# From two phases to one pipeline: normalised attention followed by a cosine MLP, on one core

## The chip, the cores and the metric

The kernel runs on one core of one Trainium2 chip. The metric is the time on the device in microseconds (us). Engines: TensorE (PE in the profile; its weight loads are PEld), VectorE (DVE), ScalarE (ACT), GpSimd (POOL) and SyncE (SP, which here only starts DMAs). Lower is better.

## The reference, cut to what matters

```python
q, k, v: (8 batches, 12 heads, 448 tokens, 64)     # float32
q_n = q / norm(q);  k_n = k / norm(k)
attn = softmax(q_n @ k_n.T / 0.1)                   # |score| <= 10
x = (attn @ v) with the heads side by side          # (3584, 768)
h = x @ w_in                                        # w_in (768, 2048)
out = (h * cos(h)) @ w_out                          # w_out (2048, 768)
```

The scores are bounded by 10, so both kernels leave out the subtraction of the maximum. The matrix products run in bf16.

## The kernel before

It has two phases, one after the other. The attention goes head by head (96 heads, loaded in 16 units of six). The keys and queries are scaled by GpSimd and transposed by TensorE. Scores are made transposed (keys on partitions), so that the exponentials can be the moving operand of the AV product. The weights of AV are 128 columns: 64 of V and 64 of ones. So partitions 64 to 127 of the result hold the softmax sum, 64 times over, and VectorE can invert and multiply.

```python
def norm(g):                         # VectorE, once per head
    vec.wait_ge(s_av, g + 1)
    vec.reciprocal(rtmp[gp].ap()[D : 2 * D, :], AV[gp].ap()[D : 2 * D, :]) ...   # 64 x 448
    vec.tensor_tensor(xt_dst, AV[gp].ap()[0:D, :], rtmp[gp].ap()[D : 2 * D, :], ALU.mult) ...

# TensorE, per head: 4 AV matmuls, 4 score matmuls of the next head, 8 transposes
for g in range(NG):
    emit_av(g)
    if g + 1 < NG: emit_sc(g + 1)
    if g + 3 < NG: emit_tp(g + 3)

# then, in a second block with its own buffers: the MLP
for sb in range(NSB + 1):            # 7 blocks of 512 tokens
    if sb < NSB: m1(sb)              # 96 matmuls of 512 columns, cos on ScalarE, product on VectorE
    if sb >= 1:  m2(sb - 1)          # 128 matmuls of 384 columns
```

## Time and profile before

The time is 840.8 us (840.4 to 840.9).

| what | value | where it is read |
|---|---|---|
| attention | 0 to about 520 us | timeline |
| MLP | about 520 to 839 us | timeline |
| VectorE busy, 130 to 330 us | 179 of 200 us | windows |
| TensorE busy, 520 to 840 us | 301 of 320 us | windows |
| reciprocals | 96 x 2.96 us = 284 us | groups |

The first two columns after the stretch in a line of the windows view are its length and TensorE's busy time. Then follow the other engines, the recorded clock, and the share and rate of the DMA engines. Kernel before:

```profile
130.00:330.00 200.00, 161.02 (x617) 70.18 (x616) 179.05 (x127) 121.41 (x142) 56.30 (x24) 1.00 0.31 81
520.00:840.00 320.00, 301.30 (x1568) 145.85 (x1568) 79.31 (x114) 101.00 (x141) 0.00 (x0) 1.00 0.12 35
```

In the attention VectorE is the full engine. In the MLP it is TensorE.

The groups show VectorE's work per head: line, engine, operation, output and input, count, then busy time in total and the mean in ns of one, then what it waited for. Kernel before:

```profile
L237 DVE RECIPROCAL rtmp<-AV 64x448 f32<-64x448 f32 x96 | 284.2, 2960 | 44.1 <-PE AV L352 39.8
L241 DVE TENSOR_TENSOR xT<-AV,rtmp 64x448 bf16<-64x448 f32 x96 | 59.3, 618 | 3.3
L228 DVE COPY qkT_sb<-TP 64x896 bf16<-64x896 bf16 x96 | 58.7, 612 | 12.7 <-PE TP L323 11.1
```

The page's slices (40 equal parts of the span, tenths of busy time; PEclk is the granted clock) for the kernel before:

```profile
PE   0797797797797797797797797999999999999997
PEclk9999999999999999999999999999999999999999
```

And its timeline of TensorE, the transposes of one head (start, length, operation; x4 is four instructions merged):

```profile
302.13 0.58 PE L319 MATMUL TP<-ident,qs 112*64 112x112 bf16 x4
302.50 0.58 PE L323 MATMUL TP<-ident,kb 112*64 112x112 bf16 x4
```

Four transposes of 112 columns take from 302.13 to 302.50, that is 1.2 columns per ns. In the MLP 128 matmuls of 384 columns take 20.80 us (chain of waits), that is 2.36 columns per ns. So the attention ran at half TensorE's rate, although the clock row reads 9 everywhere. The trace holds no clock record before 525.5 us, and the row shows full speed where nothing was recorded. **The spacing of matmuls is the better clock.**

### The profile page before, as it was taken

Reading aid. Unit: us, or ns where it says so; the run is one execution under the profiler, and the core shown is the slowest. Engines: PE = TensorE matmul, PEld = TensorE weight load, DVE = VectorE, ACT = ScalarE, POOL = GpSimd, SP = SyncE. Lnnn points to the kernel's source line nnn. Section 1 sums busy time; section 2 is a strip of 40 time slices with the busy share of each in tenths; the row PEclk is TensorE's granted clock in tenths of the full one; section 3 lists DMA queues with packets and bytes.
Section 4 is the critical chain, followed back from the end, with each engine's and each line's share of the span. In section 5 each row is a group of like instructions: output and inputs, shape, how many; then the busy total and the mean of one; then the engine's idle time right before and its main releaser. Section 6 shows DMA issues by size and latency. Waiting matters only on the chain. (4 is left out here: it accounts for less than half of the span.)

```text
span 838.7 us, 7918 instructions
## 1 busy us (share of the span) xinstructions
PE 706.1 (84%) x3104; PEld 321.0 (38%) x3104; DVE 535.0 (64%) x438; ACT 407.3 (49%) x494; POOL 132.1 (16%) x60
## 2 busy tenths in 40 slices
PE   0797797797797797797797797999999999999997
PEld 0343243243243243243333342335454444445464
DVE  3698898898898898898898898441312223131400
ACT  4656656656656656756755733442323333232311
POOL 3434124124113113213213200000000000000000
PEclk9999999999999999999999999999999999999999
DMA  9761452364033043034040000001111020102022
GB/s 286 209 198 61 115 174 80 94 174 89 10 100 99 1 98 97 3 98 98 2 99 0 1 0 1 1 0 39 38 37 39 20 56 20 57 1 76 0 76 76
DMA packets 40516, 57.13 MB, mean 68 GB/s; under 512 B 1824, under 2 KB 34080, under 8 KB 39712
## 3 DMA queue, kind: packets, MB, share of 16 engines
q1 hardware_dynamic: 40480, 56.63, 24.5%
q8 instruction: 25, 0.41, 0.2%
q14 instruction: 11, 0.09, 0.0%
HBM read 45.61 MB, written 11.01 MB: 68 GB/s over the span
## 5 line engine op out<-in xcount | busy, mean ns | idle before, releaser
L237 DVE RECIPROCAL rtmp<-AV 64x448 f32<-64x448 f32 x96 | 284.2, 2960 | 44.1 <-PE AV L352 39.8
L290 ACT ACTIVATE expT<-SCP 112x896 bf16<-112x896 f32 x192 | 165.4, 913 | 165.4 <-PE SCP L337 165.4
L337 PE MATMUL SCP<-qkT_sb 64*112 64x448 bf16 x384 | 166.8, 587 | 56.3 <-DVE qkT_sb L228 54.2
L486 DVE TENSOR_TENSOR gT<-PH,cosh 128x512 bf16<-128x512 f32 x112 | 77.5, 692 | 194.7 <-ACT cosh L459 194.7
L352 PE MATMUL AV<-expT,vp 112*128 112x448 bf16 x384 | 160.5, 572 | 35.4 <-ACT expT L290 34.3
L425 PE MATMUL PH<-xT,W 128*128 128x512 bf16 x672 | 156.5, 383 | 14.7 <-DVE gT L486 10.8
L440 PE MATMUL PO<-W,gT 128*128 128x384 bf16 x896 | 146.6, 326 | 0.0
L337 PEld LDWEIGHTS SCP<-qkT_sb 64*112 64x112 bf16 x384 | 65.7, 200 | 161.1 <-DVE qkT_sb L228 118.6
L459 ACT ACTIVATE cosh<-PH,cst 128x512 f32<-128x512 f32 x112 | 77.0, 688 | 88.3 <-PE PH L425 88.3
L440 PEld LDWEIGHTS PO<-W,gT 128*128 128x128 bf16 x896 | 87.7, 98 | 58.6
L425 PEld LDWEIGHTS PH<-xT,W 128*128 128x128 bf16 x672 | 58.2, 98 | 112.0 <-DVE gT L486 51.0
L177 POOL TENSOR_TENSOR kb<-Kf,rk 112x1536 bf16<-112x1536 f32 x16 | 44.2, 2762 | 340.9 <-ACT rk L281 340.9
L468 ACT ACTIVATE out_sb<-PO 128x768 f32<-128x768 f32 x28 | 22.7, 811 | 123.6 <-PE PO L440 123.6
L352 PEld LDWEIGHTS AV<-expT,vp 112*128 112x128 bf16 x384 | 38.4, 126 | 97.6 <-issue 55.2
L319 PE MATMUL TP<-ident,qs 112*64 112x112 bf16 x384 | 55.7, 301 | 21.7 <-POOL qs L180 21.6
L319 PEld LDWEIGHTS TP<-ident,qs 112*64 112x64 bf16 x384 | 35.3, 158 | 83.6 <-issue 83.6
L228 DVE COPY qkT_sb<-TP 64x896 bf16<-64x896 bf16 x96 | 58.7, 612 | 12.7 <-PE TP L323 11.1
L241 DVE TENSOR_TENSOR xT<-AV,rtmp 64x448 bf16<-64x448 f32 x96 | 59.3, 618 | 3.3
L323 PE MATMUL TP<-ident,kb 112*64 112x112 bf16 x384 | 55.8, 301 | 0.0
L180 POOL TENSOR_TENSOR qs<-Qf,rq 112x1536 bf16<-112x1536 f32 x16 | 44.2, 2762 | 0.0
L323 PEld LDWEIGHTS TP<-ident,kb 112*64 112x64 bf16 x384 | 43.9, 177 | 0.0
L273 ACT ACT_TABLE_LOAD x16 | 20.5, 1283 | 37.8 <-DVE qn L215 37.8
(25 smaller groups left out, 233.5 us busy)
## 6 DMA issues: line engine op xcount, KB each, us to landing
Qf<-in_q_dram SPq DMA_DIRECT2D x16, 672.0 KB, 5.5
Kf<-in_k_dram SPq DMA_DIRECT2D x16, 672.0 KB, 8.5
Vf<-in_v_dram SPq DMA_DIRECT2D x16, 672.0 KB, 9.9
wstage<-in_moe_w_in_dram SPq DMA_DIRECT2D x6, 1024.0 KB, 8.3
wstage<-in_moe_w_out_dram SPq DMA_DIRECT2D x4, 1536.0 KB, 6.7
out_dram<-out_sb SPq DMA_DIRECT2D x8, 336.0 KB, 2.6
out_dram<-out_sb SPq DMA_DIRECT2D x8, 288.0 KB, 2.6
out_dram<-out_sb SPq DMA_DIRECT2D x8, 240.0 KB, 2.5
```

The lines of the kernel that those rows point to most:

```text
L228: vec.tensor_copy(qkT_sb[gp].ap(), TP[gp].ap()).then_inc(s_ev, 1)
L237: vec.reciprocal(rtmp[gp].ap()[D : 2 * D, :], AV[gp].ap()[D : 2 * D, :]).then_inc(s_vself, 1)
L241: vec.tensor_tensor(xt_dst, AV[gp].ap()[0:D, :], rtmp[gp].ap()[D : 2 * D, :], ALU.mult).then_inc(s_dv, 1)
L290: act.activation(dst, src, ACT.Exp).then_inc(s_exp, 1)
L319: last = pe.transpose(TP[gp].ap()[0:D, NP * j : NP * (j + 1)], qs[i].ap()[:, col : col + D], ident.ap())
L323: last = pe.transpose(TP[gp].ap()[0:D, S + NP * j : S + NP * (j + 1)], kb[i].ap()[:, col : col + D], ident.ap())
L337: ins = pe.matmul(outap, lhsT, rhs, start=True, stop=True)
L352: ins = pe.matmul(AV[gp].ap(), lhsT, rhs, start=(j == 0), stop=(j == NJ - 1))
L425: ins = pe.matmul(PH[t % 2].ap(), W1v[:, c, 128 * nb : 128 * nb + 128], xTv[:, c, MB * sb : MB * sb + MB], start=(c == 0), stop=(c == NKC ...
L440: ins = pe.matmul(PO[T2 % 2].ap()[:, 512 * n2h : 512 * n2h + N2W], gTv[sbp % 2][:, f, 128 * ms : 128 * ms + 128], W2v[:, f, N2W * n2h : N2 ...
L459: act.activation(cosh[t % 2].ap(), PH[t % 2].ap(), ACT.Sin, bias=cst.ap()[:, 1:2], scale=1.0).then_inc(s_cos, 1)
L486: vec.tensor_tensor(gTv[sb % 2][:, nb, :], PH[t % 2].ap(), cosh[t % 2].ap(), ALU.mult).then_inc(s_gm, 1)
```

## The change: intent and diff

The new kernel is a small program builder (operations with the tiles that they read and write, semaphores worked out from that) and one pipeline over 16 units of six heads:

- Heads go in pairs. Scores of a pair are two 64-row tiles of the array, AV of a pair two 64-column tiles; both are meant to run side by side.
- The softmax sums come from matmuls with 32 columns of ones. ScalarE evicts AV and sums to SBUF. A gather DMA spreads a unit's 2688 sums over 128 partitions by 21 columns; VectorE adds the two halves and inverts. A DMA writes the result to DRAM, and two more read it back, copied to 64 partitions each. These three DMA steps are called the hops below.
- The MLP runs under the attention. First-layer matmuls of a batch (two units) come as one burst every second unit. Second-layer matmuls fill in by 4 to 6 in each of a unit's 12 quanta (a quantum is one score chunk of a pair). Weights are cast by the DMA.

The core of the diff, with cuts (lines of the kernel before that it takes out are those shown above):

```diff
+    def av_step(g, c):                    # one chunk of keys, both heads
+        for a in range(2):
+            r = slice(64 * a, 64 * a + 64)
+            k = slice(0, 128) if c < NC3 else r
+            ... matmul(AVv[r, 0, 0:S], vav[i][k, 8*p + (4*a + c if c < NC3 else NC3), :], px, start=(c == 0), stop=(c == NC3))
+    def av_sums(g):
+        for c in (0, 1, 2, 3):
+            for a in range(2):
+                o = slice(64 * a + 32 * (c % 2), 64 * a + 32 * (c % 2) + 32)
+                ... matmul(AVv[o, 1, 0:S], ones.ap()[k, :], px, start=(c < 2), stop=(c >= 2))
+        ... ACT Copy xuv[i][:, :, p, :] <- AVv[:, :, 0:S]
+    def gather(u):    ... 4 DMAs  sums[i] (128 x 42) <- xu
+    def recip(u):     ... DVE add of the halves, DVE reciprocal, 128 x 21
+    def spread(u):    ... DMA  scr (DRAM) <- rcp
+    def broadcast(u): ... 2 DMAs  RB (64 partitions each) <- scr
+    def normalise(u, p): ... DVE xT <- xu * RB
...
+            if u == 0 and kq >= 2 or u == 1:
+                load_w(1)                                  # POOL's DMA queue, with the cast
...
+            if per_quantum:
+                m2_fill(per_quantum[kq % len(per_quantum)])
+            if g >= 1:
+                if c in (1, 2):
+                    av_step(g - 1, 2 * c - 2)
+                    av_step(g - 1, 2 * c - 1)
+                if c == 2: av_sums(g - 1)
+                if kq == 3: gather(u - 1)
+            if u % 2 == 1 and u >= 3 and kq == M1_AT:       # M1_AT = 2
+                m1((u - 3) // 2)
...
+            fills = (4,) if b % 2 == 0 else (6, 5, 5)
```

## The prediction

> **What bounds the kernel now.** The windows view splits the 838.7 us span: 0-30 us start, 30-520 us attention, 520-839 us MLP. In 330-520 us VectorE is busy 173.5 of 190 us: attention is VectorE-bound. Per head (groups): reciprocal over 64 partitions 2960 ns, eviction of transposes 612, multiply 618, plus 3.5 us of reductions per unit; in all about 4.8 us x 96 heads. In the MLP TensorE is the chain (chain of waits: L440 17%, L425 11% of the span); 128 second-layer matmuls take 20.8 us (162 ns each, 384 columns), a 12-matmul pair of first-layer groups 2.97 us where 12 x 216 ns would be 2.6.
>
> The timeline also shows 448-column attention matmuls starting 373 ns apart (1.2 columns/ns), though the page says granted clock 1.0; the MLP streams 384 columns in 162 ns (2.4 columns/ns). The Trainium skill ("TensorE: Matmul & The Clock Gate", part 1) describes a half-rate state until the array has been busy for some 3.4 us; this trace agrees with the rates: attention, with TensorE never saturated, runs at half.
>
> **What the change does.**
> - Removes the 2960 ns reciprocal (284 us in total): 16 small ones over 21 columns instead, plus two hops through DRAM that have several us of slack.
> - VectorE per pair: eviction 0.61, reduction about 1.1, normalise 0.62; MLP multiplies 64 x 1.09, output evictions 56 x 0.5. Total about 220 us (535 now).
> - ScalarE: per pair 3 x 0.91 + 0.54 exponentials and 0.91 eviction, 4.2 us, 201 us; sines 64 x 1.0; table loads about 17 x 1.28 (66 now). About 300 us.
> - GpSimd: squares, scaling, casts about 3.7 us per pair, 180 us, below ScalarE.
> - The MLP runs under the attention, so TensorE becomes the bound, and stays at full rate.
>
> **TensorE, estimated at 2.4 columns/ns.** MLP 768 x 189 ns + 896 x 162 ns = 291 us. Per pair: 7 transposes 0.5; scores and AV as two concurrent tiles each, 0.8 + 0.8; sums 0.65; about 2.75 us. Tile-shape switches: the trace's gaps from one matmul kind to the next are 0.12-0.18 us at half rate; I take 0.08 x 13 per pair = 1.05. So 3.8 x 48 = 182 us. That tiles overlap is from the skill ("TensorEngine Tiling (Array Packing)", Tiling Modes, key properties); no trace yet shows it. If they don't, pairs cost 1.8-2 us more, about +90 us.
>
> Sum: first scores 10; TensorE 473; three first units without MLP work, limited by ScalarE or by a half-rate TensorE, +12; waiting for weights (18 MB wanted in 55 us) +4; bubbles round seven first-layer bursts (score buffers shared, table loads) 14; DRAM round trip of the last unit less its filling 4; last store 3; small stalls 10. About **530 us**, range **480-610**. Faster by over 2%: 0.96; within 2%: 0.02; slower: 0.02.
>
> **What would show it right.** TensorE busy in nearly every slice after the first 50 us; 384-column matmuls 162 ns apart from then; the two matmuls of a score or AV pair starting a few ns apart; VectorE about 40% busy, ScalarE about 55%; TensorE the chain of waits; GpSimd never waited for after the second unit; no long VectorE wait on the broadcast.
>
> **What would make it wrong.** Tiles not overlapping, or dearer switches (600 or more). The clock falling back to half rate between bursts: 448 columns again 373 ns. Weight loads through GpSimd's queue delaying the first MLP burst or the loads of units 2 and 3. The DRAM hops being slower than the five quanta given to them, which stalls VectorE, then the single output bank, then TensorE. If switches are nearly free and bubbles small, 480.

## The result, and the profile after

The median is 593.2 us (590.8 to 599.0, four runs) against 840.8 us before. The ratio is 0.7064, 95% interval 0.7029 to 0.7098. Ratios here are the mean time of one kernel's fast runs over that of the other's of the same rounds, so not quite the ratio of the medians quoted beside them.

The page's busy times and slices of the kernel after:

```profile
PE 491.1 (83%) x3152; PEld 217.4 (37%) x3152; DVE 234.7 (40%) x300; ACT 290.9 (49%) x358; POOL 192.0 (33%) x159
PE   1380366989998999899898999889898999896997
PEclk9996597999999999999999999999999999998999
DMA  6699777015800852045701761145702320122013
```

VectorE went from 535 us to 235 us. From the eighth slice on TensorE is nearly full. The first seven slices (103 us) are weaker, but for the third, and in them the DMA engines are busy.

TensorE's timeline of one pair in the steady state of the kernel after:

```profile
146.99 0.82 PE L477 MATMUL PO<-W,gT 128*128 128x384 bf16 x4
147.75 0.36 PE L347 MATMUL SC<-qkT 64*128 64x448 bf16 x2
148.04 0.82 PE L477 MATMUL PO<-W,gT 128*128 128x384 bf16 x4
148.80 0.36 PE L347 MATMUL SC<-qkT 64*128 64x448 bf16 x2
149.10 0.56 PE L331 MATMUL TP<-ident,qks 128*128 128x128 bf16 x7
149.50 0.81 PE L477 MATMUL PO<-W,gT 128*128 128x384 bf16 x4
150.24 0.57 PE L368 MATMUL AV<-PX,va 128*64 128x448 bf16 x4
150.74 0.36 PE L347 MATMUL SC<-qkT 64*128 64x448 bf16 x2
151.04 0.82 PE L477 MATMUL PO<-W,gT 128*128 128x384 bf16 x4
151.79 0.69 PE L368 MATMUL AV<-PX,va 128*64 128x448 bf16 x4
152.41 0.85 PE L380 MATMUL AV<-PX,ones 128*32 128x448 bf16 x8
153.19 0.38 PE L351 MATMUL SC<-qkT 64*64 64x448 bf16 x2
153.50 0.82 PE L477 MATMUL PO<-W,gT 128*128 128x384 bf16 x4
```

From 146.99 to 153.50 is one pair: 6.51 us, of which 16 second-layer matmuls of 162 ns are 2.60, so 3.91 us belong to the attention of two heads. Two score matmuls of 448 columns go through in 0.29 us (147.75 to 148.04); one after the other they would need 0.37 us for the columns alone, at 2.4 per ns. So the tiles do run side by side: unmerged, the trace has the two scores starting 4 ns apart (147.749 and 147.753) and the first two of AV 3 ns apart (150.241 and 150.244).

Where the start loses its time is seen in two lines of the kernel after, one of GpSimd's timeline (its squares of unit 2) and one of TensorE's (the first MLP burst), with the wait and its releaser in brackets:

```profile
59.31 4.95 POOL L294 TENSOR_TENSOR sq<-raw 128x896 bf16<-128x896 f32 x3 [20.43 <-DMA raw<-in_k_dram]
97.80 6.87 PE L432 MATMUL SC<-xT,W 128*128 128x448 bf16 x24 [4.21 <-DVE xT L418]
```

The inputs of unit 2 were asked for at 27 us and used at 59. The first burst began at 97.8 us. Bursts then come every 65.1 us on average (97.8 to 488.2 us, six steps). Around the second burst TensorE waits twice (kernel after):

```profile
160.78 2.44 PE L432 MATMUL AV<-xT,W 128*128 128x448 bf16 x12 [1.01 <-ACT xu L383]
181.39 1.15 PE L477 MATMUL PO<-W,gT 128*128 128x384 bf16 x6 [1.98 <-DVE gT L437]
```

The first group of this burst uses the AV buffer before ScalarE has emptied it. Behind the burst, nothing of the second layer is ready.

### The profile page after: what moved, and what is told of

It reads as the page before. It is cut to its first block, busy times and chain, and to the rows that moved or that the text cites. A ratio compares the mean times of both kernels' runs of the same rounds, so it can differ in the third digit from the quotient of the medians.

```text
span 589.0 us, 7661 instructions
## 1 busy us (share of the span) xinstructions
PE 491.1 (83%) x3152; PEld 217.4 (37%) x3152; DVE 234.7 (40%) x300; ACT 290.9 (49%) x358; POOL 192.0 (33%) x159
## 4 chain that ended last, share of the span: by engine, by line
PE 68%; DMA 15%; DVE 6%; SPq 6%; POOL 2%; ACT 2%; issue 2%; DVEq 0%; ACTq 0%
PE PO L477 20%; PE SC L432 17%; PE AV L432 9%; DMA raw<-in_k_dram 6%; PE AV L368 6%; DMA RB<-scr 5%; PE AV L380 4%; PE SC L347 4%; PE TP L331 3%; PE SC L477 2%; DVE osb L485 2%; DMA sums<-xu 2%; POOL sq L294 2%; PE SC L351 2%; DVE gT L437 1%
## 5 line engine op out<-in xcount | busy, mean ns | idle before, releaser
L355 ACT ACTIVATE PX<-SC 128x896 bf16<-128x896 f32 x144 | 131.2, 918 | 84.8 <-PE SC L347 83.4
L315 POOL TENSOR_TENSOR qks<-raw,rn 128x896 bf16<-128x896 f32 x47 | 79.4, 1689 | 253.5 <-ACT rn L309 253.5
L432 PE MATMUL SC<-xT,W 128*128 128x448 bf16 x516 | 104.4, 359 | 4.2 <-DVE xT L418 4.2
L294 POOL TENSOR_TENSOR sq<-raw 128x896 bf16<-128x896 f32 x47 | 80.5, 1739 | 29.3 <-DMA raw<-in_k_dram 29.3
L347 PE MATMUL SC<-qkT 64*128 64x448 bf16 x288 | 53.8, 373 | 34.0 <-ACT PX L355 23.6
L437 DVE TENSOR_TENSOR gT<-SC,cosb 128x896 bf16<-128x896 f32 x43 | 47.0, 1092 | 69.7 <-ACT cosb L435 69.7
L383 ACT ACTIVATE xu<-AV 128x896 f32<-128x896 f32 x48 | 44.0, 917 | 55.9 <-PE AV L380 55.9
L432 PEld LDWEIGHTS SC<-xT,W 128*128 128x128 bf16 x516 | 50.9, 99 | 53.8 <-issue 9.2
L299 DVE TENSOR_REDUCE n<-sq 128x14 f32<-128x896 bf16 x48 | 50.7, 1078 | 31.1 <-POOL sq L294 26.9
L368 PE MATMUL AV<-PX,va 128*64 128x448 bf16 (+1 forms) x384 | 61.9, 380 | 0.0
L432 PE MATMUL AV<-xT,W 128*128 128x448 bf16 x252 | 53.4, 364 | 7.2 <-DVE xT L418 5.2
L418 DVE TENSOR_TENSOR xT<-xu,RB 128x448 bf16<-128x448 f32 x48 | 38.2, 808 | 51.3 <-DMA RB<-scr 51.3
```

Source lines behind the costliest of these rows:

```text
L294: P.op(eng, lambda e: e.tensor_tensor(sq[j].ap(), src, src, ALU.mult), [("raw", i, p)], [("sq", j)])
L299: P.op("DVE", lambda e: e.tensor_reduce(out=n2[i].ap()[:, p * 2 * NS : (p + 1) * 2 * NS], in_=sq[j].ap().rearrange("p (x d) -> p x d", d=D ...
L315: P.op(eng, lambda e: e.tensor_tensor(qksv[i][:, :, h, :].rearrange("p s h d -> p h s d"), rawv[i][:, h, :, :], bass.AP(rn[i], p * 2 * NS, ...
L347: P.op("PE", lambda e, r=r, a=a, rhs=rhs: e.matmul(sc[:, a, 0:S], qkT[j].ap()[r, S + TL + 128 * c : S + TL + 128 * c + 128], rhs, start=Tr ...
L355: P.op("ACT", lambda e: e.activation(PXm[j][:, c], sc[:, :, 0:S], ACT.Exp, scale=1.0 / TAU), ["SC%d" % z], [("PX", j, c)])
L368: P.op("PE", lambda e, r=r, k=k, a=a, px=px: e.matmul(AVv[r, 0, 0:S], vav[i][k, 8 * p + (4 * a + c if c < NC3 else NC3), :], px, start=(c ...
```

## The experiments

Twelve more kernels ran. "m1(0)" below is the start of the first MLP burst, read from TensorE's timeline; it is given where the argument uses it.

| run | median us | ratio to before | m1(0) us |
|---|---|---|---|
| after | 593.2 | 0.7064 | 97.8 |
| w_later | 592.5 | 0.7056 | 96.3 |
| lump | 596.8 | 0.7100 | 97.6 |
| av_full (wrong result) | 605.5 | 0.7204 | 98.2 |
| recip_dve | 604.9 | 0.7201 | 98.1 |
| no_w (wrong result) | 581.3 | 0.6915 | 84.3 |
| w_split | 583.9 | 0.6947 | 84.6 |
| lump_first | 569.4 | 0.6763 | 97.6 |
| before_norecip (wrong result) | 797.1 | 0.9482 | |
| before_burst (wrong result) | 804.5 | 0.9569 | |
| refilled | 555.1 | 0.6595 | 98.4 |
| no_hops | 563.0 | 0.6686 | 70.5 |
| no_hops_late | 530.3 | 0.6318 | 71.0 |

### Where the gain comes from: the reciprocal alone, in the kernel before

```diff
-vec.reciprocal(rtmp[gp].ap()[D : 2 * D, :], AV[gp].ap()[D : 2 * D, :])
+vec.tensor_scalar(rtmp[gp].ap()[D : 2 * D, :], AV[gp].ap()[D : 2 * D, :], 1e-6, None, ALU.mult)
```

> The kernel before with its reciprocal replaced by a multiplication by a constant of the same shape (wrong result on purpose, 0.6 us in place of 2.96): what the reciprocal alone is worth without any overlap of attention and MLP. VectorE then needs about 2.4 us per head. Theory A (the array then is dense enough for its clock to rise): heads at 2.5-2.9 us, total 600-660 us. Theory B (attention stays at the half clock, where the head's matmuls take 3.7 us plus 0.45 of gaps): heads at 4.2 us, total 760-790.

It took 797.1 us: theory B, 7 us above its range. Taking 96 x 2.33 us from the engine that was full saved only 43.7 us. TensorE's timeline of this kernel shows why:

```profile
301.48 1.74 PE L337 MATMUL SCP<-qkT_sb 64*112 64x448 bf16 x4
303.15 0.58 PE L319 MATMUL TP<-ident,qs 112*64 112x112 bf16 x4
303.52 0.58 PE L323 MATMUL TP<-ident,kb 112*64 112x112 bf16 x4
305.64 1.74 PE L337 MATMUL SCP<-qkT_sb 64*112 64x448 bf16 x4
```

In the middle of a unit a head now takes 4.16 us (301.48 to 305.64). The transposes still go four in 0.37 us, so the clock is still at half. Eight matmuls of 448 and eight of 112 columns are 3.73 us at 1.2 columns per ns, 90% of the head. Over 130 to 330 us, changes of unit included, a head takes 4.76 us on average (672 matmuls, 16 per head), against 5.19 in the kernel before (617). Behind VectorE stood a half-speed TensorE, almost as slow.

### Can a burst of dense work raise the clock, and does attention keep it?

In before_norecip, once, at the eleventh head:

```diff
+                    if g == 10 and j == 0:
+                        for _ in range(40):
+                            pe.matmul(AV[gp].ap(), lhsT, rhs, start=True, stop=True)
```

> before_norecip (the kernel before without its reciprocal; wrong result on purpose) with 40 extra matmuls of the AV kind, back to back, once, at the eleventh head; their output is overwritten. In before_norecip the attention ran at the half clock although TensorE was busy near 90% of it. Theory A (an uninterrupted stretch of several us raises the clock, and traffic as dense as this attention's keeps it): from the burst on 448-column matmuls come 190 ns apart, heads take some 2.5 us, total 640-680 us. Theory B (this attention's pattern can't hold the full clock): at most a few us around the burst are fast, total 797-815 us.

It took 804.5 us: theory B. The slices (clock row) and TensorE's timeline of before_burst:

```profile
PEclk9999855555555555555555557999999999999999
```

```profile
75.67 9.01 PE L354 MATMUL AV<-expT,vp 112*128 112x448 bf16 x40
88.24 0.96 PE L337 MATMUL SCP<-qkT_sb 64*112 64x448 bf16 x4
91.12 0.96 PE L337 MATMUL SCP<-qkT_sb 64*112 64x448 bf16 x4
94.28 0.54 PE L355 MATMUL AV<-expT,vp 112*128 112x448 bf16 x2 [1.69 <-ACT expT L290]
96.53 1.74 PE L337 MATMUL SCP<-qkT_sb 64*112 64x448 bf16 x4 [0.90 <-DVE qkT_sb L228]
```

The clock records of this trace say: full from 78.27 us, half from 95.34, full from 491.3, where the MLP is. (The 9s in the row before 78 us are again stretches without a record.) The burst did raise the clock, and two heads then took 2.88 us each. In such a head TensorE streams only 1.87 of 2.88 us, 65%, and the clock held through both. It fell eleven us after the burst, at the change of unit, where the exponentials came late: in the 3.41 us before the fall TensorE streamed about 1.1 us, a third. Then it stayed at half for 396 us. So this attention did not raise the clock by itself, and lost it again at the next change of unit.

In the kernel after, the records show full clock from 102 us to the end, except for 3.4 us at 249, 6.8 us at 539 and the last 2. But that is not the MLP's doing alone. The records also show full clock from 30.6 to 47.6 us, and the first MLP matmul comes at 97.8. TensorE's timeline of the kernel after, the last score matmuls of two pairs that follow each other:

```profile
31.18 0.38 PE L351 MATMUL SC<-qkT 64*64 64x448 bf16 x2
35.68 0.38 PE L351 MATMUL SC<-qkT 64*64 64x448 bf16 x2
```

A pair takes 4.50 us there, 2.25 per head, with no MLP under it. In the 3.41 us before 30.6 TensorE streamed 80% of the time (columns at 1.2 per ns). Why that raised the clock, and 90% in before_norecip did not, was not tested; one difference is that the old scores use 64 of the array's rows at a time and the new ones run in twos.

What loses the clock can be worked out from the kept traces, with each matmul's columns at 2.4 per ns and tiles side by side counted once. All 86 falls that the 14 traces record follow a stretch of 3.413 us in which TensorE streamed at most 39% of the time. In the 1805 such stretches after which the full clock went on, it streamed at least 36%.

### Do the column tiles of AV run at the same time?

```diff
-    AVv[r, 0, 0:S], vav[i][k, 8*p + (4*a + c if c < NC3 else NC3), :], px, start=(c == 0), stop=(c == NC3)
+    # main chunks: 128 columns of weights, out on 128 partitions, both heads into one sum (wrong result)
+    AVv[o, 0, 0:S], vav[i][k, xs, :], px, start=(c == 0 and a == 0), stop=(c == NC3)
```

> Wrong result on purpose: the six main AV matmuls of a pair use 128 columns of weights over the whole array in place of two 64-column tiles side by side; counts and streamed columns are the same, the two tails stay as they are. Theory A (the two column tiles run at the same time): six matmuls of 0.19 us one after the other in place of three slots, +0.56 us per pair, less one or two shape changes saved (0.1 us each): +15 to +27 us, so 605-622 us. Theory B (tiles don't overlap): no more than 0.5% change or faster by the saved changes.

It took 605.5 us, 12.3 more. TensorE's timeline of av_full, to be held against 150.24 to 150.74 above:

```profile
151.38 0.92 PE L370 MATMUL AV<-PX,va 128*128 128x448 bf16 x4
152.24 0.36 PE L347 MATMUL SC<-qkT 64*128 64x448 bf16 x2
```

Four AV matmuls need 0.86 us as full-width ones and 0.50 us as tiles. A pair goes from 6.51 to 6.83 us (148.23 to 155.06). Times the 39 pairs of the units that run under the MLP that is 12.5 us, the whole difference. Theory A: the tiles overlap. But the saving is small beside 248 us.

### Is the spreading of the sums needed?

recip_dve makes the sums on 64 partitions per head, inverts 128 x 448 per pair on VectorE and drops the three DMA hops:

```diff
-    ones = sb("ones", [128, 32], BF16)
+    ones = sb("ones", [128, 64], BF16)
-                o = slice(64 * a + 32 * (c % 2), 64 * a + 32 * (c % 2) + 32)
+                o = slice(64 * a, 64 * a + 64)
...
-                if kq == 6: recip(u - 1); spread(u - 1)
-                if kq == 8: broadcast(u - 1)
+                if kq in (6, 8, 10): head_recip(u - 1, (kq - 6) // 2)     # DVE reciprocal, 128 x 448
```

> Undoes the spreading of the sums, right result: sums are made on 64 partitions per head (64-column weights of ones), VectorE inverts 128x448 per pair (about 2.96 us, 142 us in all, VectorE then at 62% of the span) and the gather, spread and broadcast DMAs go. Theory A (spreading is needed: a 3 us reciprocal in VectorE's queue holds back the evictions of the single output bank and so TensorE): +25 to +60 us, 615-650 us, with longer waits of second-layer matmuls for the output eviction. Theory B (VectorE has slack enough once TensorE is the bound, and the DRAM hops cost the same or more): within 1.5% of 593 or up to 10 us faster by the last unit's round trip.

It took 604.9 us. That is 2% more, between the two theories, and not for the reason of theory A: TensorE's waits for the output eviction are as before (17.4 us in 28 waits, against 16.0 in 22). Part of it is on TensorE: eight sum matmuls with 64 columns of weights need 0.90 us where those with 32 needed 0.78. A pair goes from 6.51 to 6.66 us, which over 39 pairs is 6 us. The other 6 us fit the end of the run: the last burst waited 11.4 us for VectorE in place of 5.2, as the last unit's three reciprocals stood before it (542.42 to 552.41). So in this schedule the spreading was worth 2%, although it takes 136 us of reciprocals from VectorE: once TensorE was the bound, VectorE had room for them. One reciprocal of 448 columns takes 2.94 us on 128 partitions and 2.96 on 64; one of 21 columns takes 0.29. The columns count, not the partitions.

### What holds the first burst?

Two edits of one line, and a third run:

```diff
-            if u == 0 and kq >= 2 or u == 1:
+            if u == 1 and 3 <= kq < 9 or u == 2 and kq >= 3:     # w_later
+            if u == 1 and 3 <= kq < 9 or u == 3 and kq < 4:      # w_split
```

no_w leaves the lines where they are and puts a memset of VectorE in the place of each weight load.

> The ten weight loads are issued later, behind the loads of units 2 and 3 (six from the middle of unit 1, four from the middle of unit 2); nothing else changes. Theory A (weights and the inputs of unit 2 share the DMA engines, busy 96% from 15 to 60 us, so unit 2 waits until 59 us for its inputs): unit 2's squares start near 37 us in place of 59, the first MLP burst near 65-75 us in place of 98, and the whole takes 560-572 us in place of 593. Theory B (the input loads are slow by themselves, by their runs of 768 and 256 bytes and their issue): unit 2's inputs still land after 52 us and the whole is within 1.5% of 593, or later weights delay the first burst just as much.

w_later gained nothing (592.5 us). Its first half came true, and more: the squares of unit 2 started at 31.8 us, not 59.3. But the burst still began at 96.3. VectorE's timeline of w_later:

```profile
49.94 0.66 DVE L399 TENSOR_TENSOR rcp<-sums 128x21 f32<-128x21 f32 x1 [8.54 <-DMA sums<-xu]
66.12 1.16 DVE L418 TENSOR_TENSOR xT<-xu,RB 128x448 bf16<-128x448 f32 x2 [14.72 <-DMA RB<-scr]
83.00 3.84 DVE L399 TENSOR_TENSOR rcp<-sums 128x21 f32<-128x21 f32 x1 [11.14 <-DMA sums<-xu]
```

The weights now met the hops of the sums. VectorE took its instructions in the order of the program and stood still for them (8.5, 14.7 and 11.1 us), and the eviction of the next pair's transposes stood behind.

> Wrong result on purpose: no weight is read from memory; the weight tiles are set to a constant by VectorE at the places where the loads were issued (some 2 us each, while VectorE idles). Theory A (before the first MLP burst the kernel is bound by what the DMA engines have to move; the weights take 33 us of all 16 engines): the first burst starts 25-40 us earlier, at 58-73 us in place of 98, and the whole takes 553-570 us. Theory B (prelude bound by the pair pipeline or by the hops of the sums): first burst still after 85 us, total over 580.

> First-layer weights from the middle of unit 1, behind the inputs of unit 2, second-layer weights only at the first MLP burst (unit 3). In the run with all weights later, units 1 and 2 started earlier but the sums' hops waited behind W2 and other loads (8.3 us for the gather, 6 for the spread, 8.6 for the broadcast) and the burst came at 96 us as before. Theory A (DMA throughput before the burst): taking W2's 17 us of the engines out of that stretch moves the burst to 76-84 us and the whole to 573-582 us. Theory B (the order of the queue matters, not its sum): no more than 5 us gained.

Without any weight traffic the burst began at 84.3 us and the whole took 581.3. With the second-layer weights held back to the burst, it began at 84.6 us and the whole took 583.9 us, with the right result. The gain of no_w, 12 us, is half of the least that its theory A asked, and its total falls under theory B. The 9 us of w_split are 2 short of its theory A and more than its theory B allowed. So DMA throughput is a part of it (in the kernel after the DMA engines were 96% busy from 15 to 60 us, and by the trace's DMA records the weight loads alone took 33 us of all sixteen). It is not the whole: in w_split the burst still waited until 84 us, 5.3 us of it for VectorE, which had stood 6.6 us for the last hop. no_w says less than it was meant to: its memsets (21 us) did not fall into idle time but held up the evictions of the transposes, so that the fifth pair's last scores came at 55.9 us, against 42.9 in w_later. And the hops alone are not the cause either: recip_dve has none, with the weights where they were, and its burst began at 98.1.

### Fewer changes of tile shape

```diff
-            fills = (4,) if b % 2 == 0 else (6, 5, 5)
+            fills = (0, 16, 0, 0) * 3 if b % 2 == 0 else (0, 16, 0, 0, 0, 16, 0, 16, 0, 16, 0, 0)      # lump
+            fills = (16, 0, 0, 0) * 3 if b % 2 == 0 else (16, 0, 0, 0, 16, 0, 16, 0, 16, 0, 0, 0)      # lump_first
-            if c == 1 and g + 1 < NG:
+            if c == 0 and g + 1 < NG:                                                                  # lump_first
                 transposes(g + 1)
```

> Second-layer matmuls are placed in whole groups of 16 right behind the transposes (same 128x128 tile shape) in place of 4 to 6 in every quantum. Theory A (each change of tile shape costs TensorE about 0.1 us, and a group start waits for the eviction of the single output bank): 4 changes fewer per pair over 39 pairs save 16 us, and output-bank waits and the wait behind each first-layer burst save 15-25 us: 555-570 us. Theory B (the gaps come from ScalarE's pace, or evening out the fill is what keeps ScalarE fed): no gain, 590-610 us, with more waiting of the scores for the exponentials.

lump lost 3.5 us (596.8). The saving came back as a new wait, in TensorE's timeline of lump:

```profile
149.31 0.36 PE L347 MATMUL SC<-qkT 64*128 64x448 bf16 x2
150.52 0.36 PE L347 MATMUL SC<-qkT 64*128 64x448 bf16 x2 [0.85 <-ACT PX L358]
```

Three scores now follow each other, there are two score buffers, and ScalarE has an eviction and an exponential to do first.

> Second-layer matmuls in whole groups of 16 with the transposes directly behind a pair's first scores. In the first lumped run each pair had 4 shape changes fewer (6.51 us less 0.26 us) but TensorE waited 0.85 us per pair for the exponential of the tail, because three scores followed each other with two score buffers. Here 2.6 us of second-layer work stands between them. Theory A: the wait goes, three or so shape changes (0.065 us each) fewer per pair and fewer waits for the output bank: pairs at 6.3 us in place of 6.5, total 575-587. Theory B (what is saved on the array comes back as another wait): 590-600.

lump_first took 569.4 us, 24 less than the kernel after; a little better than expected. From its TensorE timeline:

```profile
197.75 0.36 PE L347 MATMUL SC<-qkT 64*128 64x448 bf16 x2
198.45 2.76 PE L477 MATMUL PO<-W,gT 128*128 128x384 bf16 x16
203.94 0.36 PE L347 MATMUL SC<-qkT 64*128 64x448 bf16 x2
```

A pair takes 6.19 us (197.75 to 203.94) in place of 6.51, with three changes of shape fewer: 0.11 us each. In lump a pair took 7.10 us, but its second scores came 1.21 us after the first (149.31 to 150.52), where 448 columns at 2.4 per ns need 0.19. Less these 1.02 us of waiting it is 6.08: four changes fewer saved 0.43 us, again 0.11 each. (The 0.065 of the expectation takes the wait as the bracket's 0.85 us, which starts only at the modelled end of the matmul.) The Trainium skill says in "TensorEngine Tiling (Array Packing)", Tiling Modes, key properties, that changing the tiling mode drains TensorE; it gives no figure. The other part of the 24 us, some 11, is near what TensorE's waits for the output bank lost, 16.0 us in the kernel after and 1.4 in lump_first; the two parts were not tested apart.

### Towards a better version

refilled puts lump_first and the weight order of w_split together, with five more edits: the first burst in quantum 7 of unit 3 in place of 3; the first unit's sums inverted and broadcast later in the queue; two groups of the second layer kept back for behind a burst; the first-layer groups taking SC1, SC0, AV in turn in place of a running rotation; one more group in the tail.

```diff
+            at = {3: (8,)}.get(u, (0, 4, 8) if u % 2 == 0 else (0, 3, 8) if b % 2 == 0 else (0, 3, 5, 8, 10))
+            fills = tuple(16 if kq in at else 0 for kq in range(12))
-        name, ph = PHs[nph[0] % 3]
+        name, ph = PHs[gidx % 3]                  # PHs = SC1, SC0, AV
-            ... and kq == M1_AT
+            ... and kq == (6 if u == 3 else M1_AT)
```

> A version meant to beat both, right result: lump_first, plus the weight order of w_split, plus the first MLP burst moved from the third to the seventh quantum of unit 3 (attention goes on while its input is finished), plus the first unit's sums inverted and broadcast later in VectorE's queue, plus two second-layer groups kept back so that something is ready behind each burst, plus first-layer groups taking the score buffers first and in the order in which they come free. Expected if the waits named so far are the ones that count: lump_first's 569 us less 10 (weights), less up to 3 us for each of seven bursts, less 3 in the tail: 530-548 us. If the savings overlap or come back as other waits: 550-565.

It took 555.1 us, 14 less than lump_first: the range given for savings that overlap. The bursts now come every 60.2 us (98.4 to 459.8, six steps; 62.2 in lump_first). The start was again not better (98.4 us, and in the middle of this burst TensorE waited 6.7 us for VectorE). VectorE's and GpSimd's timelines of refilled show a second cause:

```profile
100.54 10.13 DVE L399 TENSOR_TENSOR rcp<-sums 128x21 f32<-128x21 f32 x1 [2.99 <-DMA sums<-xu]
```

```profile
101.28 1.70 POOL L315 TENSOR_TENSOR qks<-raw,rn 128x896 bf16<-128x896 f32 x1
102.92 0.61 POOL L322 CAST va<-vraw 128x512 bf16<-128x512 f32 x1
103.49 1.69 POOL L315 TENSOR_TENSOR qks<-raw,rn 128x896 bf16<-128x896 f32 x1
105.12 0.60 POOL L322 CAST va<-vraw 128x512 bf16<-128x512 f32 x1
105.69 4.94 POOL L294 TENSOR_TENSOR sq<-raw 128x896 bf16<-128x896 f32 x3
```

An addition of 21 columns that takes 0.17 or 0.18 us in eight of its sixteen places in this trace, and up to 1.46 in the others, took 10.13 us here: from 100.54 until GpSimd's row of instructions ended at 110.63. In w_later the add of 83.00 ended at 86.84, within 0.05 us of GpSimd's squares. The Trainium skill says this in "SBUF — State Buffer", Terms: VectorE and GpSimd share a port pair, held exclusively for the whole instruction, and the loser is fully blocked. These traces agree, and show that a waiting VectorE instruction of two SBUF inputs may lose to several GpSimd instructions in a row.

no_hops then removes the hops altogether, with the sums of recip_dve placed next to the AV matmuls of the same shape, the weights behind the inputs of unit 2, the bursts one unit earlier, and each pair's reciprocal behind the output eviction (the order of the second layer is that of refilled):

```diff
+            if c == 1 and g >= 2:
+                head_recip((g - 2) // UP, (g - 2) % UP)
+                normalise((g - 2) // UP, (g - 2) % UP)
...
-            if u % 2 == 1 and u >= 3 and kq == M1_AT: m1((u - 3) // 2)
+            if u % 2 == 0 and u >= 2 and kq == 7:     m1((u - 2) // 2)
```

> Right result. In the refilled version the first MLP burst was still late (after 100 us): the hops of the sums took 13.5 us (gather), 6 (spread) and 7-9 us (broadcast) among the loads, and the burst needs them. Here the sums are made on 64 partitions per head and inverted by VectorE at each pair (as in recip_dve, which cost 12 us where nothing else was changed), so no MLP input goes through DRAM; the burst of a batch then comes one unit earlier (units 2, 4, 6...); the sums with 64-column weights share the tile shape of the AV matmuls and follow them directly (three shape changes fewer per pair); weights behind the inputs of unit 2; second-layer groups of 16 and two of them kept back as in refilled. Theory A (the hops under DMA load are what holds the first burst, and a 3 us reciprocal per pair fits VectorE's slack when it is placed behind the output eviction): first burst at 52-68 us, pairs with a group at 6.0-6.3 us, total 505-530 us. Theory B (the prelude is held by the loads themselves, or VectorE's reciprocals hold back evictions): first burst after 80 us or pairs over 6.6 us, total over 540.

It took 563.0 us. Neither theory: the first burst came at 70.5 us, 27 us earlier than in the kernel after, and a pair took 6.05 us. These 27 us belong to the hops, the weights and the earlier place together. But the bursts had a new wait, in TensorE's waits of no_hops (us in total, times, longest):

```profile
PE SC L439 <- DVE xT L425: 36.8, 7, 11.0
```

The reciprocals stood just before each burst in VectorE's queue. (Of the first wait, 11.0 us, only a part is theirs: VectorE had stood 6.2 us for GpSimd's squares.) The clock records of this trace drop to half around each of these bursts, for 3.4 to 10.2 us. The last run moves the bursts four quanta later and nothing else but the places of the fills:

```diff
-            if u % 2 == 0 and u >= 2 and kq == 7:
+            if u % 2 == 0 and u >= 2 and kq == 11:
-            at = {2: (), 4: (0, 8, 10)}.get(u, (0, 4, 8) if b % 2 == 0 else (0, 4, 6, 8) if u % 2 else (0, 4, 8, 10))
+            at = {2: (), 3: (4, 8), 4: (0, 4)}.get(u, (0, 4, 8) if (u - 3) // 2 % 2 == 0 else (0, 4, 6, 8))
```

> no_hops with each first-layer burst four quanta later (twelfth quantum of units 2, 4, 6...), right result. In no_hops pairs with a group took 6.05 us as wished, but each of seven bursts waited 4 to 5 us (11 the first) for VectorE, whose reciprocals came just before it, and behind such a wait the clock was at half rate for 6.8 us. Theory A (those waits, and the clock they cost, are what no_hops lost): waits of the bursts under 1.5 us, some 37 us of waits and 7 x 3 us of slow clock mostly gone, total 515-535 us. Theory B (VectorE, with the reciprocals at 64% of the span, has no slack where the burst now comes either): waits stay, total over 550.

It took 530.3 us (528.0 to 535.3), ratio 0.6318, with the right result: theory A, 11% below the changed kernel and 37% below the kernel before. The wait for the MLP input is gone from the list of TensorE's waits, and after 70.7 us the clock is recorded at half only for 6.8 us at 470. Its page:

```profile
PE 471.7 (89%) x3152; PEld 230.8 (44%) x3152; DVE 366.5 (69%) x316; ACT 283.1 (54%) x358; POOL 197.7 (37%) x159
```

So the spreading of the sums, which gains 2% in the changed kernel as it stands, is not part of the fastest version found. No run has this version with the spreading, so what it would cost here is not shown; in refilled it put three hops and a two-input addition between the attention and the burst.

## Why the prediction was right or wrong

It gave 530 us with a range of 480 to 610 and 96% for faster; measured were 593 us. The direction and most of the mechanism held; the middle value was 63 us low. Point by point:

- **VectorE as the bound of the attention, half clock behind it: right.** The prediction took the reciprocal as the thing removed. before_norecip shows that removing it alone, from the old attention, is worth 44 us. The other 204 us came with everything else at once: heads in pairs, a new order, and the MLP under the attention. How they share it is not shown. No run has the new attention first and the MLP after it. An estimate from the traces: 31 us to the second pair, 46 pairs at 4.50 us and 320 us of MLP make 558 us, if the loads keep up, and that is less than 593. So the overlap, which the prediction relied on for the full clock, is not shown to be what brought the gain.
- **Tiles overlap: right** (av_full; 0.29 us for a pair of score matmuls). It set 90 us on the case that none of the tiles overlap. Only the six main AV matmuls of a pair were tested, at 12 us.
- **Cost of a pair on TensorE: right in size.** 3.8 us predicted, 3.91 measured. A change of shape was put at 0.08 us, measured 0.11.
- **VectorE 40%: right** (40%). **ScalarE about 55%**: 49%. **TensorE the chain: right** (68% of the chain of waits). Two of its own signs failed: TensorE was not busy in nearly every slice after 50 us, but only after 103, and VectorE did wait for the broadcast, 51.3 us in 15 waits.
- **The start: the term that was mis-sized.** The prediction had "first scores 10", "three first units without MLP work ... +12" and "waiting for weights (18 MB wanted in 55 us) +4". With nine pairs at 3.8 us that puts the first burst at 60 us; it came at 97.8, 38 us later. It named weight loads as a risk and then priced them at 4 us. The windows view of before had the number to check with: 254 GB/s at 83% busy engines in the first 30 us, in longer runs of data than the new ones (1.4 KB per packet, 0.8 in the kernel after). An estimate from that is 306 GB/s at best, so 18 MB need 59 us before any hop is served. (The kernel after then moved 193 GB/s at 96% from 15 to 60 us.) And it gave the hops "several us of slack" by the steady state, where the start is what they hold up. w_later, w_split and recip_dve show the weights and the hops one behind the other: taking away either alone leaves the burst at 84 us or later, and with the weights later and the hops gone it comes at 70.5 (no_hops, where it also stands earlier).
- **"Bubbles round seven first-layer bursts ... 14" and "small stalls 10": too small.** By the prediction's own terms a batch needs 36.4 us of MLP matmuls, 22.8 of pairs and about 3.2 of bubbles and stalls (its 24 us over the steps), 62.4 in all. Measured were 65.1, so six steps cost 16 us more. lump_first takes a step to 62.2 and refilled to 60.2: changes of shape, output-bank waits, the order of the burst's buffers and a missing reserve of second-layer work, not tested one by one.

The two terms are 54 of the 63 us that the prediction was short. What stays open: how much of the last 9 us lies in the tail, how the gain divides between the new attention and the overlap, and what it takes to raise the clock.

## What to carry to other kernels

Before removing the fullest engine's work, look at what stands right behind it, and at what rate: here a half-clock TensorE, which only showed in the spacing of its matmuls. When a change both rewrites a phase and merges it with another, run the rewritten phase unmerged too: here that run is missing, and the early pairs of the kernel after hint that the rewritten attention keeps the clock up by itself. In an in-order pipeline, count each wait from the place where it stands in the queue: a cheap DMA hop or a 3 us instruction is free in one position and holds up everything in another.

## What the Trainium skill lacked or had wrong

- "TensorE: Matmul & The Clock Gate", Part 1, tells of a half rate until about 3.4 us of sustained activity, and of a fall after idle time. It gives no busy share that keeps the full rate without a true idle stretch. Here all 86 recorded falls followed a stretch of 3.413 us with at most 39% streamed, and the rate was kept with 36% or more; 90% at half rate never raised it in the old attention (before_norecip), 80% did in the new one. The recorded durations are whole multiples of 3.413 us (17.067, 6.827), but for the last of each trace, as the page's window of 3413 ns has it.
- The same part warns that the clock records of a trace can be unreliable and asks for a cross-check, but neither it nor any other page says that a stretch without records may be a half-rate stretch. Here 525 us without records read as full speed.
- "TensorEngine Tiling (Array Packing)" says that a change of mode drains the array but has no cost for it: 0.11 us per change here at full clock.
- "SBUF — State Buffer" has the exclusive port pair of VectorE and GpSimd. It was not drawn on for the prediction. What could be added is the size: a 0.17 us addition held for 10.13 us by seven GpSimd instructions in a row.
